# Eight-head retention and a gated MLP on one core: q scaled before its transpose, half-array matmuls, and an order of work computed in the kernel

## The chip, the core and the metric

The kernel runs on one core of a Trainium2 chip. A core has a matrix engine (TensorE, "PE" in the profile; its weight loads are listed as "PEld" and can run beside matmuls), a vector engine (VectorE, "DVE"), a scalar engine (ScalarE, "ACT"), a general engine (GpSimd, "POOL") and SyncE ("SP"), which here only issues transfers. The engines run in parallel, each takes its own instructions in the order of its own list, and they wait for one another on semaphores. The metric is the device time of one execution in microseconds (us): the median of several executions.

## The reference

Batch 8, 8 heads, 576 positions, 64 channels per head. The first half is retention: attention without softmax, in which the score of query position t and key position s is multiplied by gamma^(t-s) for s up to t and by zero above. The second half is a gated MLP that mixes positions with a 576x576 matrix.

```python
scores = scale * np.matmul(q, k.transpose(0, 1, 3, 2))
gamma = 1.0 - 2.0 ** (-5.0 - np.arange(H, dtype=np.float32))
Dmat = np.where(rel >= 0, gamma[:, None, None] ** rel[None, :, :], 0.0)
x = np.matmul(scores * Dmat[None], v)          # then heads side by side: 512 channels
...
h = gelu(x @ w_in)                             # 1024 wide, tanh form
u, v = (h[..., :512], h[..., 512:])
v_n = (v - mean) / np.sqrt(var + 1e-06) * g_ln
v_s = np.einsum('ts,bsd->btd', w_sg, v_n) + b_sg[None, :, None]
return x + (u * v_s) @ w_out
```

## The kernel before

Two batches form a pair of 1152 positions, cut into 9 tiles of 128 positions; there are 4 pairs, so 36 tiles. Tile 4 of a pair (m == MID) holds the last 64 positions of one batch and the first 64 of the next. gamma^(t-s) is split into a factor of t and a factor of s, so that no 576x576 decay matrix is needed: v is multiplied by gamma^(-s) (`gv`, line 220), and the output by gamma^t and the scale (`ttab`, line 275). Earlier tiles enter through a running sum of k^T v per head, kept in a bank of PSUM (`zp`, line 289) and copied out after each tile (`zbd`).

The work of a tile, by line:

- `load` (73 to 75): q, k and v of the tile, 256 KB each in float32, by SP, into a ring of five buffers.
- `prep` (217, 220): POOL casts q and k to bf16 (`qkb`) and multiplies v into `vpad`, where the 64 columns of each head lie in a block of 128 whose other half is zero.
- `attn_T` (234 to 239): PE transposes q and k into one PSUM tile; DVE copies q out (`qT`), and ACT and DVE copy one half each of k into a block-diagonal `kbd`, with zeros in the other half of the rows.
- `attn_S` (251, 253): eight 128x128 matmuls give the scores, each with a contraction of 128 rows of which 64 hold zeros; DVE multiplies by the triangle (`ret`).
- `attn_O` (267, 271, 275): four matmuls from the running sum and eight from `vpad`, all on the whole array; DVE multiplies by `ttab` into `xT`.
- `attn_Z` (289 to 293): the running sum is extended and copied out by DVE and ACT.
- `mlp_V` (307 to 326): four 512-wide matmuls; ACT applies gelu (`vg`), DVE takes mean and variance (`bst`, `mv`), POOL forms the inverse root (`rs`) and the offset (`nm`), ACT normalises into `vn`.
- `mlp_U` (336, 339): sixteen matmuls, gelu on ACT into `uT`.
- `mlp_W` (349, 354): once the five tiles of one batch have their `vn`, the mixing with `w_sg`: per 128 channels, five steps that alternate between two PSUM tiles of 288 positions; DVE multiplies by `uT` into `gT`.
- `mlp_O` (361, 364, 367, 368): eight matmuls per tile, a copy by ACT, and a 256 KB store that ACT's own queue issues.

PSUM has eight banks: one each for `tp`, `ot` and `zp`, two for scores, three (`psD`) shared by `hv`, `hu`, `wp` and `op`. The program issues the functions in a loop over tiles with fixed offsets (prep two tiles ahead, the MLP one behind, two pieces of `mlp_W` or `mlp_O` per turn), and the framework's own scheduler then places the instructions on each engine. `w_sg` is loaded by POOL with a cast (line 190) and transposed by PE in ten groups (`build_wT`, line 205); each of these groups ends with one matmul that uses 64 rows of the array. Rows for g_ln and b_sg are prepared by small DVE operations (lines 97 to 121).

Of the kernel before, what the change touches and what calls it, by code (L numbers as in the profile page):

```python
# [11 lines left out]
F32 = mybir.dt.float32  # L12
# [3 lines left out]
Alu = mybir.AluOpType  # L16


@with_exitstack
def kernel(  # L20
# [18 lines left out]
    NP = B // 2  # L39
    MID = NT // 2  # L40
    HS = S // 2
    SB = (S + 127) // 128
    ORG = S // 2
    lng = [math.log(1.0 - 2.0 ** (-5.0 - i)) for i in range(H)]
# [3 lines left out]
    ld = ctx.enter_context(tc.tile_pool(name="ld", bufs=5))  # L48
    work = ctx.enter_context(tc.tile_pool(name="work", bufs=4))
    pairp = ctx.enter_context(tc.tile_pool(name="pairp", bufs=2))  # L50
    vnp = ctx.enter_context(tc.tile_pool(name="vnp", bufs=10))
    psA = ctx.enter_context(tc.tile_pool(name="psA", bufs=1, space=bass.MemoryType.PSUM))
    psS = ctx.enter_context(tc.tile_pool(name="psS", bufs=2, space=bass.MemoryType.PSUM))
    psD = ctx.enter_context(tc.tile_pool(name="psD", bufs=3, space=bass.MemoryType.PSUM))


    def segs(m):

        if m < MID:
            return [(0, 0, 128 * m, 128)]  # L60
        if m == MID:
            return [(0, 0, 128 * m, S - 128 * m), (S - 128 * m, 1, 0, 128 * (m + 1) - S)]
        return [(0, 1, 128 * m - S, 128)]

    loaded = {}

    def load(i):
        p, m = divmod(i, NT)
        qk = ld.tile([128, 2, H, D], F32, name="qk", tag="qk")
        vf = ld.tile([128, H, D], F32, name="vf")  # L70
        for (p0, b, r0, n) in segs(m):
            bb = 2 * p + b
            nc.sync.dma_start(qk[p0:p0 + n, 0, :, :], q[bb, :, r0:r0 + n, :].transpose([1, 0, 2]))
            nc.sync.dma_start(qk[p0:p0 + n, 1, :, :], k[bb, :, r0:r0 + n, :].transpose([1, 0, 2]))
            nc.sync.dma_start(vf[p0:p0 + n, :, :], v[bb, :, r0:r0 + n, :].transpose([1, 0, 2]))
        loaded[i] = (qk, vf)

    load(0)


    w_in = consts.tile([128, KK, 2 * F2], BF, name="w_in")
    w_out = consts.tile([128, KK, DM], BF, name="w_out")
    wnat = consts.tile([128, SB, S + 128], BF, name="wnat")
    g_col = consts.tile([128, KK], F32, name="g_col")
    w_stage = []
    for half in (1, 0):
        for c in (0, 2):
            wst = ld.tile([128, 2, F2], F32, name="wst", tag="qk")
            nc.sync.dma_start(wst[:], moe_w_in.rearrange("(c p) f -> p c f", p=128)[:, c:c + 2, half * F2:(half + 1) * F2])
            w_stage.append((half, c, wst))  # L90
        load(1 if half else 2)
    nc.sync.dma_start(g_col[:], moe_g_ln.rearrange("(c p) -> p c", p=128))

# [5 lines left out]
    g_tmp = consts.tile([128, KK], F32, name="g_tmp")  # L101
    nonzero(g_col[:], g_tmp[:])
    row4 = consts.tile([4, 2, S], F32, name="row4")
    row4b = consts.tile([4, 2, S], BF, name="row4b")
    row_t = consts.tile([4, S], F32, name="row_t")
    nc.sync.dma_start(row4[:, 0, :F2], moe_g_ln.partition_broadcast(4))
    nc.sync.dma_start(row4[:, 1, :], moe_b_sg.partition_broadcast(4))
    sel_i = consts.tile([4, 1], I32, name="sel_i")
    nc.gpsimd.iota(sel_i[:], pattern=[[0, 1]], base=0, channel_multiplier=1)
    sel = consts.tile([4, 3], F32, name="sel")  # L110

    def build_rows():
        nonzero(row4[:, 0, :F2], row_t[:, :F2])
        nc.vector.reciprocal(row4[:, 0, :F2], row4[:, 0, :F2])
        nc.vector.tensor_copy(sel[:, 0:1], sel_i[:])
        nc.vector.tensor_scalar(sel[:, 1:2], sel[:, 0:1], 2.0, -1.0, op0=Alu.is_ge, op1=Alu.mult)
        nc.vector.scalar_tensor_tensor(sel[:, 2:3], sel[:, 1:2], -2.0, sel[:, 0:1], op0=Alu.mult, op1=Alu.subtract)
        for a, n in ((0, F2), (1, S)):
# [3 lines left out]
        for t in vmid:  # L122
            nc.sync.dma_start(t[0][NB0:NB0 + 4, :], row4b[:, 0, :F2])
            nc.sync.dma_start(t[1][0:4, :], row4b[:, 0, :F2])
        nc.sync.dma_start(wT[0][SB - 1][NB0:NB0 + 4, :], row4b[:, 1, :])
        nc.sync.dma_start(wT[1][0][0:4, :], row4b[:, 1, :])


    ident = consts.tile([128, 128], BF, name="ident")
    make_identity(nc, ident[:])  # L130
    tri = consts.tile([128, 128], BF, name="tri")
    nc.gpsimd.memset(tri[:], 1.0)
    nc.gpsimd.affine_select(tri[:], tri[:], pattern=[[1, 128]],
                            compare_op=Alu.is_ge, fill=0.0, base=0, channel_multiplier=-1)
    tri_mid = consts.tile([128, 128], BF, name="tri_mid")
    NB0 = S - 128 * MID
    nc.vector.tensor_copy(tri_mid[:], tri[:])
    nc.vector.memset(tri_mid[:NB0, NB0:], 0.0)

# [67 lines left out]


    st = {}
    xTs, uTs, gTs = {}, {}, {}  # L210
    zp = {}

    def prep(i):
# [245 lines left out]
```

## Time and profile before

| | us |
|---|---|
| median of 3 runs (273.85 to 275.9) | 273.96 |
| the profiled execution: its span, first to last instruction | 272.1 |
| median less the span: what lies around it | 1.86 |
| PE busy | 227.3 |
| DVE busy | 189.2 |
| ACT busy | 130.1 |
| POOL busy | 128.1 |

The page of the profile gives the busy time of each engine, and the span in 40 slices with the busy share in tenths. Other views group instructions by line (count, busy time, mean duration, and what ended the idle time before them), list the waits, list instructions in order of time, or give the busy time in stretches that the reader chooses. Matmuls are pipelined: the duration of one is longer than the distance from its start to the start of the next, and the latter is what PE can deliver. Of the profiled execution itself no time but the span is given, so the 1.86 us around it are taken from the median.

### The profile page before, as it was taken

To read this page: it belongs to the slowest core of one execution; us is meant where nothing else is said; L and a number is where in the kernel's file an instruction comes from. 1 tells how busy PE (TensorE), PEld (TensorE's weight loads), DVE (VectorE), ACT (ScalarE), POOL (GpSimd) and SP (SyncE) were. 2 spreads that over 40 slices of the span, in tenths; PEclk is the share of its full clock that TensorE was granted. 3 is DMA by queue.
4 is the path that set the end of the run, shared out by engine and by line. 5 is a ranking of instruction groups with operands and counts; after the bars stand their busy time and mean duration, and the time that the engine had idled before them with its cause. 6 is when DMAs were issued, how large, how long until landed. Compare 5 with 4: busy or idle time off the path is not lost.

```text
span 272.1 us, 6371 instructions
## 1 busy us (share of the span) xinstructions
PE 227.3 (84%) x2498; PEld 171.3 (63%) x2498; DVE 189.2 (70%) x405; ACT 130.1 (48%) x230; POOL 128.1 (47%) x244
## 2 busy tenths in 40 slices
PE   0477747869899899987999899879998999889893
PEld 0245534647577687665877677657767877667561
DVE  7766797767786687656865886568777876687140
ACT  1632522344245545554465445565455476644612
POOL 7835316465267456664635575348544551131100
PEclk9999595999999999999999999999999999999998
DMA  7999999099403799398949789596966022100314
GB/s 167 273 290 232 221 198 229 4 209 193 83 4 104 200 219 213 111 279 214 193 119 211 166 168 263 167 225 126 221 173 149 2 77 80 40 4 0 116 62 173
DMA packets 120606, 42.02 MB, mean 154 GB/s; under 512 B 113824, under 2 KB 114424, under 8 KB 120576
## 3 DMA queue, kind: packets, MB, share of 16 engines
q1 hardware_dynamic: 114736, 31.51, 57.6%
q10 hardware_dynamic: 5184, 9.44, 9.5%
q0 software_dynamic: 656, 0.66, 1.4%
q8 instruction: 19, 0.31, 0.6%
q14 instruction: 11, 0.09, 0.1%
HBM read 32.80 MB, written 9.44 MB: 155 GB/s over the span
## 4 chain that ended last, share of the span: by engine, by line
PE 39%; DVE 22%; ACT 11%; DMA 8%; POOL 7%; issue 6%; SPq 3%; ACTq 2%; POOLq 0%; DVEq 0%
PE hv L307 7%; PE wp L349 6%; PE op L361 6%; PE hu L336 5%; DVE bst L312 5%; DMA vf<-in_v_dram 4%; ACT ob L367 4%; DVE xT L275 4%; ACT vg L310 4%; PE tp L234 3%; PE sc L251 3%; PE ot L271 3%; POOL rs L317 2%; ACTq L368 2%; DVE kbd_169 L239 2%
## 5 line engine op out<-in xcount | busy, mean ns | idle before, releaser
L316 POOL TENSOR_SCALAR rs<-mv 128x1 f32<-128x1 f32 x36 | 8.0, 223 | 110.0 <-DVE mv L314 105.1
L326 ACT ACTIVATE vn<-vg,nm,rs 128x512 bf16<-128x512 f32 x32 | 26.0, 814 | 50.7 <-POOL nm L319 50.7
L253 DVE TENSOR_TENSOR ret<-sc,tri 128x512 bf16<-128x512 f32 x64 | 41.0, 682 | 10.9 <-PE sc L251 10.9
L307 PE MATMUL hv<-w_in,xT 128*128 128x512 bf16 x144 | 40.3, 398 | 3.8 <-DVE xT L275 3.7
L217 POOL CAST qkb<-qk 128x1024 bf16<-128x1024 f32 x36 | 37.2, 1032 | 10.8 <-DMA qk<-in_k_dram 7.1
L312 DVE BATCH_NORM_STATS2 bst<-vg 128x6 f32<-128x512 f32 x36 | 25.0, 694 | 24.7 <-ACT vg L310 24.0
L336 PE MATMUL hu<-xT,w_in 128*128 128x128 bf16 x576 | 38.8, 221 | 1.3 <-ACT ob L367 1.3
L310 ACT ACTIVATE vg<-hv 128x512 f32<-128x512 f32 x36 | 21.5, 597 | 36.6 <-PE hv L307 30.5
L336 PEld LDWEIGHTS <-w_in 128*128 128x128 bf16 x576 | 35.1, 99 | 4.0 <-issue 2.5
L361 PE MATMUL op<-w_out,gT 128*128 128x512 bf16 x144 | 36.9, 379 | 0.0
L349 PEld LDWEIGHTS <-vn 128*128 128x128 bf16 x256 | 24.4, 97 | 18.9 <-issue 11.8
L354 DVE TENSOR_TENSOR gT<-wp,uT 128x288 bf16<-128x288 f32 x64 | 26.1, 448 | 11.3 <-PE wp L349 11.3
L234 PEld LDWEIGHTS <-qkb 128*128 128x128 bf16 x288 | 20.2, 103 | 15.5 <-POOL qkb L217 7.5
L234 PE MATMUL tp<-ident,qkb 128*128 128x128 bf16 x288 | 23.7, 229 | 6.7 <-POOL qkb L217 6.5
L275 DVE TENSOR_TENSOR xT<-ot,ttab 128x512 bf16<-128x512 f32 x36 | 24.9, 691 | 6.1 <-PE ot L271 5.4
L367 ACT ACTIVATE ob<-op 128x512 f32<-128x512 f32 x36 | 21.1, 592 | 11.2 <-PE op L364 7.2
L339 ACT ACTIVATE uT<-hu 128x512 bf16<-128x512 f32 x36 | 21.2, 590 | 10.3 <-PE hu L336 10.2
L317 POOL TENSOR_TENSOR rs<-rs,mhalf 128x1 f32<-128x1 f32 x36 | 20.6, 571 | 2.7
L307 PEld LDWEIGHTS <-xT 128*128 128x128 bf16 x144 | 12.5, 101 | 12.9 <-DVE xT L275 5.2
L236 DVE COPY qT<-tp 128x512 bf16<-128x512 bf16 x36 | 15.0, 417 | 7.2 <-PE tp L234 6.9
L361 PEld LDWEIGHTS <-gT 128*128 128x128 bf16 x144 | 12.7, 98 | 8.8 <-DVE gT L354 0.3
L364 PEld LDWEIGHTS <-xT 128*128 128x128 bf16 x144 | 11.1, 98 | 8.4
(135 smaller groups left out, 440.9 us busy)
## 6 DMA issues: line engine op xcount, KB each, us to landing
out_dram<-ob ACTq DMA_DIRECT2D x36, 256.0 KB, 2.2
qk<-in_q_dram SPq DMA_DIRECT2D x32, 256.0 KB, 4.8
qk<-in_k_dram SPq DMA_DIRECT2D x32, 256.0 KB, 4.6
vf<-in_v_dram SPq DMA_DIRECT2D x32, 256.0 KB, 4.9
wst<-in_moe_w_in_dram SPq DMA_DIRECT2D x4, 512.0 KB
wst<-in_moe_w_out_dram SPq DMA_DIRECT2D x2, 512.0 KB
qk<-in_q_dram SPq DMA_DIRECT2D x8, 128.0 KB, 5.8
qk<-in_k_dram SPq DMA_DIRECT2D x8, 128.0 KB
```

What stands on the lines that cost most here:

```text
L217: nc.gpsimd.tensor_copy(qkb[:], qk[:].rearrange("p a h d -> p a (h d)"))
L234: nc.tensor.transpose(tp[:, a, kk, :], s["qkb"][:, a, kk * 128:(kk + 1) * 128], ident[:])
L253: nc.vector.tensor_tensor(ret[:, 4 * j:4 * j + 4, :], sc[:], msk[:].unsqueeze(1).to_broadcast([128, 4, 128]), op=Alu.mult)
L275: nc.vector.tensor_tensor(xTs[p][:, :, 128 * m:128 * m + 128], ot[:], ttab[:, :, t0:t0 + 128], op=Alu.mult)
L307: nc.tensor.matmul(hv[:], xTs[p][:, kk, 128 * m:128 * m + 128], w_in[:, kk, F2:], start=(kk == 0), stop=(kk == KK - 1))
L310: nc.scalar.activation(vg[:], hv[:], Act.Gelu_apprx_tanh)
L312: nc.vector.bn_stats(bst[:], vg[:])
L336: nc.tensor.matmul(hu[:, c, :], w_in[:, kk, 128 * c:128 * c + 128], xTs[p][:, kk, 128 * m:128 * m + 128], start=(kk == 0), stop=(kk == KK ...
L349: nc.tensor.matmul(ps[half][:], vns[t0 + j][e][:, 128 * c:128 * c + 128], wT[e][j][:, half * HS:(half + 1) * HS], start=(j == 0), stop=(j ...
L354: nc.vector.tensor_tensor(gTs[p][:, c, col:col + HS], ps[half][:], uTs[p][:, c, col:col + HS], op=Alu.mult)
L361: nc.tensor.matmul(op[:], gTs[p][:, c, r], w_out[:, c, :], start=(c == 0), stop=False, skip_group_check=True)
L367: nc.scalar.activation(ob[:], op[:], Act.Copy)
```

## The change

The attention half is rewritten, several operations move to other engines, and the order of all instructions is computed in the kernel.

- q is multiplied by gamma^t and the scale before it is transposed (`qs`, on POOL), so the output needs no `ttab`; ACT copies it to `xT`. k is cast by ACT (`kb`) rather than by POOL.
- The transposed q and k are copied out of PSUM by one DVE operation of 1024 columns (`qkT`). There is no block-diagonal k: the scores of even heads use rows 0 to 63 of the array, those of odd heads rows 64 to 127, and the two write different PSUM banks.
- v is not padded: an even head's output uses columns 0 to 63 of the array, an odd head's columns 64 to 127, so they write the two halves of one PSUM tile.
- The running sum is copied out by ACT alone. The normalisation `vn` moves from ACT to POOL, as (vg - mean) * rs, and the addition of 1e-6 from POOL to DVE.
- The mixing forms one half of 288 positions after the other, each in a bank of its own; the product overwrites `uT`.
- Stores are issued by SP, in one list with the loads; `w_sg` is loaded by SP as float32 and cast by ACT.
- The framework's scheduler is switched off (`tc.manual_schedule()`). The kernel describes each piece of work as a unit with an engine, a cost, a key (a due time, in steps of 5300 ns per tile), what it reads and writes, and the PSUM banks it takes. The class `Plan` then plays the units through: at each step it takes the engine that can start first and, among that engine's units that can start by then, the one with the lowest key. Instructions are emitted in that order.

```diff
+    def emit(self):
...
+        for _ in units:
+            t, e = min((max(free[e], min(start(n) for n in r)), e) for e, r in ready.items() if r)
+            n = min((m for m in ready[e] if start(m) <= t), key=lambda m: (units[m][2], m))
...
+            free[e] = t + cost
+            done = t + cost + self.HOP[e]
...
+            emit(*([[s[1] for s in held[n]]] if take is not None else
+                   [[held[m][w][1] for m, which in give for w in which]] if give is not None else []))
...
+        plan.add("ACT", 600, key + 1, lambda: nc.scalar.activation(
+            kb[a][:], qkf[l][:, 1, :, :].rearrange("p h d -> p (h d)"), Act.Copy),
+                 reads=rd(i, 1), writes=[("kb", a)])
+        plan.add("POOL", 1220, key, lambda: nc.gpsimd.tensor_tensor(
+            qs[a][:].rearrange("p (h d) -> p h d", h=H), qkf[l][:, 0, :, :], gq[:, m, :].unsqueeze(2).to_broadcast(bc), op=Alu.mult),
+            reads=rd(i, 0) + ["gq"], writes=[("qs", a)])
+        plan.add("POOL", 1220, key + 2, lambda: nc.gpsimd.tensor_tensor(
+            vb[a][:], vf[l][:], gv[:, m, :].unsqueeze(2).to_broadcast(bc), op=Alu.mult),
+            reads=rd(i, 2) + ["gv"], writes=[("vb", a)])
...
+        plan.add("DVE", 650, key, lambda banks: nc.vector.tensor_copy(
+            qkT[r][:].rearrange("p a k c -> p (a k c)"), banks[0][:]),
+            reads=[("tpu", i)], writes=[("qkT", r)], give=[(u, [0])])
...
-            for r in range(4):
-                kk, hh = 2 * j + r // 2, r % 2
-                nc.tensor.matmul(sc[:, r, :], s["kbd"][:, kk, hh, :], s["qT"][:, kk, :],
-                                 start=True, stop=True, skip_group_check=True)
+            for kk in range(KK):
+                for hh in range(2):
+                    sl = slice(hh * 64, hh * 64 + 64)
+                    nc.tensor.matmul(banks[hh][:, kk, :], qkT[r][sl, 1, kk, :], qkT[r][sl, 0, kk, :],
+                                     start=True, stop=True, skip_group_check=True)
...
-            for hh in range(2):
-                nc.tensor.matmul(ot[:, kk, :], s["vp"][:, 2 * kk + hh, :], s["ret"][:, 2 * kk + hh, :],
-                                 start=first, stop=(hh == 1), skip_group_check=True)
+            for kk in range(KK):
+                for hh in range(2):
+                    nc.tensor.matmul(ot[hh * 64:hh * 64 + 64, kk, :], vb[a][:, 2 * kk + hh, :], ret[r][hh][:, kk, :],
+                                     start=(m == 0 and kk == 0), stop=True, skip_group_check=True)
...
-        nc.vector.tensor_tensor(xTs[p][:, :, 128 * m:128 * m + 128], ot[:],
-                                ttab[:, :, t0:t0 + 128], op=Alu.mult)
+        plan.add("ACT", 600, key + 8, lambda banks: nc.scalar.activation(
+            xT[p % NX][:, :, 128 * m:128 * m + 128], banks[0][:], Act.Copy),
+            reads=[("otu", i)], writes=[("xT", p % NX, m)], give=[(u, [0])])
...
-            nc.scalar.activation(vn[:], vg[:], Act.Identity, scale=rs[:], bias=nm[:])
+            nc.gpsimd.tensor_tensor(st[:, 8:9], st[:, 8:9], mhalf[:], op=Alu.pow)
...
+                nc.gpsimd.tensor_scalar(dst[sl, :], vg[g][sl, :], st[sl, 6:7], st[sl, 8:9],
+                                        op0=Alu.subtract, op1=Alu.mult)
...
-                nc.tensor.matmul(ps[half][:], vns[t0 + j][e][:, 128 * c:128 * c + 128],
-                                 wT[e][j][:, half * HS:(half + 1) * HS],
...
+                        nc.tensor.matmul(banks[0][:, :HS], src[:, 128 * c:128 * c + 128],
+                                         wT[e][j][:, half * HS:(half + 1) * HS],
...
-        nc.scalar.dma_start(outf[128 * i:128 * i + 128, :], ob[:])
+            plan.add("SP", 400, key, lambda i=i: nc.sync.dma_start(outf[128 * i:128 * i + 128, :], ob[i % NO][:]),
+                     reads=[("ob", i % NO)], writes=[("out", i)], dma=720)
...
+    with tc.manual_schedule():
+        plan.emit()
```

More of the change, by code (lines that the diff above doesn't have):

```diff
@@ L54, with sb @@
[L54 removed]
+    psum = ctx.enter_context(tc.tile_pool(name="psum", bufs=1, space=bass.MemoryType.PSUM))
+    def sb(name, shape, dt=BF):
+        return consts.tile(shape, dt, name=name)
+    NL, NQ, NR, NX, NO, NG = 5, 3, 3, 2, 4, 4
+    qkf = [sb(f"qkf{i}", [128, 2, H, D], F32) for i in range(NL)]
+    vf = [sb(f"vf{i}", [128, H, D], F32) for i in range(NL)]
+    qs = [sb(f"qs{i}", [128, H * D]) for i in range(NQ)]
@@ L78 @@
[L78 to L91, printed above, removed]
@@ new lines @@
+    tables()
+    g_and_b()
+    for n, (half, c) in enumerate(((1, 0), (1, 2), (0, 0), (0, 2))):
+        w_load(half, c, n)
+    load(0)
+    for i in range(N):
+        if i:
+            load(i)
+        if i == 2:
+            weights()
+        attention(i)
+        if i:
+            mlp_V(i - 1)
+            mlp_U(i - 1)
+        if i and (i - 1) % NT == MID:
+            batch(2 * ((i - 1) // NT))
+        if i and (i - 1) % NT == NT - 1:
+            batch(2 * ((i - 1) // NT) + 1)
+    mlp_V(N - 1)
```

595 lines of the change are left out of this document (318 added, 277 removed).

## The prediction

> **What bounds the kernel now.** The page comes first, then the stretches of the span, then PE's instructions in order of time.
>
> ```profile
> span 272.1 us, 6371 instructions
> PE 227.3 (84%) x2498; PEld 171.3 (63%) x2498; DVE 189.2 (70%) x405; ACT 130.1 (48%) x230; POOL 128.1 (47%) x244
> ```
>
> ```profile
> 0.00:20.00 20.00, 7.50 (x52) 5.25 (x53) 14.32 (x41) 8.13 (x17) 13.09 (x30) 1.00 1.03 244
> 20.00:45.00 25.00, 15.91 (x154) 11.83 (x152) 21.17 (x40) 7.66 (x14) 9.67 (x16) 0.80 1.07 221
> 45.00:75.00 30.00, 24.59 (x271) 18.27 (x272) 21.26 (x45) 12.01 (x22) 15.16 (x26) 0.94 0.71 130
> 75.00:250.00 175.00, 162.65 (x1896) 125.63 (x1895) 127.96 (x272) 94.51 (x166) 88.24 (x168) 1.00 0.65 145
> 250.00:272.10 22.10, 16.69 (x130) 10.32 (x128) 4.46 (x11) 7.75 (x13) 1.90 (x6) 0.96 0.29 108
> ```
>
> The columns are the stretch, its length, busy time (and count) of PE, PEld, DVE, ACT and POOL, granted clock, DMA share, GB/s. There are two kernels in one span. From 75 us to 250 us PE is busy 162.65 of 175. Before 75 us it is busy 48.0 of 75, while the DMA engines are full (1.03, 1.07) until 45 us: there it waits for data and for chains. So the questions are how much PE work there is, how early PE fills, and how much it loses once full. The work is read from starts that follow without a gap:
>
> ```profile
> 130.85 0.39 PE L289 MATMUL zp<-vpad_164,qkb 128*128 128x128 bf16 x4
> 131.08 0.41 PE L349 MATMUL wp<-wT_0_191,vn 128*128 128x288 bf16 x2
> ...
> 132.30 0.29 PE L349 MATMUL wp<-wT_0_191,vn 128*128 128x288 bf16 x1
> ...
> 133.81 0.61 PE L251 MATMUL sc<-qT,kbd_169 128*128 128x128 bf16 x8
> 134.25 1.03 PE L307 MATMUL hv<-w_in,xT 128*128 128x512 bf16 x4
> 135.12 0.61 PE L234 MATMUL tp<-ident,qkb 128*128 128x128 bf16 x8
> 135.56 1.06 PE L336 MATMUL hu<-xT,w_in 128*128 128x128 bf16 x16
> 136.46 0.22 PE L267 MATMUL ot<-qT,zbd_170 128*128 128x128 bf16 x1
> ...
> 137.12 1.03 PE L361 MATMUL op<-w_out,gT 128*128 128x512 bf16 x4
> ...
> 138.21 0.38 PE L361 MATMUL op<-w_out,gT 128*128 128x512 bf16 x1
> ```
>
> Start to start: running sum 0.23 us, scores 0.44, hv 0.87, transposes 0.44, hu 0.90, output 0.66 (12 matmuls at 0.055), op 1.09, and ten wp in 1.22 (131.08 to 132.30). The 36 tiles of scores, hv, transposes, hu and op make 36 x 3.74 = 134.6; outputs 32 x 0.66 + 4 x 0.44 (a pair's first tile has no running sum) = 22.9; sums 32 x 0.23 = 7.4; 320 wp 39.0. The ten groups that transpose w_sg take 0.46 each:
>
> ```profile
> 64.19 0.52 PE L205 MATMUL wtp<-ident,wnat 128*128 128x128 bf16 x5
> 64.65 0.30 PE L349 MATMUL wp<-wT_2_193,vn 128*128 128x288 bf16 x1
> ```
>
> That is 4.6. **PE's work is 208.5 us** at the full clock; the other 63.6 of the span are waiting, clock and edges.
>
> **The change, part by part.** *Half-array matmuls.* Scores and the v part of the output are eight 0.055 us matmuls each. If the two halves of each pair run at once, a tile saves 0.22 on either: 36 x 0.44 = 15.8. If they run one after the other they save nothing. No row of this trace shows two halves at work; I take the full saving, since nothing but their place differs from matmuls that follow one another, and keep the other end for the range. Their cost stands in the 0.46 above. Its fifth matmul is the one that uses 64 rows:
>
> ```profile
> L205 PE MATMUL wtp<-ident,wnat 64*128 64x64 bf16 x10 | 2.1, 209 | 0.0
> ```
>
> Four at 0.055 and one of half the columns would be 0.25, so going to half the rows and back costs 0.21, 0.105 per switch. In the compiled order of the changed kernel the array's shape changes 156 times: 20 in the w_sg groups, which exist before too, and 136 new ones (some outputs stand next to scores and share one). 136 x 0.105 = 14.3; the low end is 0, if eight matmuls hide what one could not. I take the row. PE's work is then 208.5 - 15.8 + 14.3 = **207.0**: the halves pay for their own switches and no more. The Trainium skill, "TensorEngine Tiling (Array Packing)", Key Properties, says that different tiles of the array can load weights and multiply in parallel; no run here shows that yet, and by it the full saving holds.
>
> *What moves between engines*, from rows grouped by line:
>
> ```profile
> L253 DVE TENSOR_TENSOR ret<-sc,tri 128x512 bf16<-128x512 f32 x64 | 41.0, 682 | 10.9 <-PE sc L251 10.9
> L354 DVE TENSOR_TENSOR gT<-wp,uT 128x288 bf16<-128x288 f32 x64 | 26.1, 448 | 11.3 <-PE wp L349 11.3
> L326 ACT ACTIVATE vn<-vg,nm,rs 128x512 bf16<-128x512 f32 x32 | 26.0, 814 | 50.7 <-POOL nm L319 50.7
> L312 DVE BATCH_NORM_STATS2 bst<-vg 128x6 f32<-128x512 f32 x36 | 25.0, 694 | 24.7 <-ACT vg L310 24.0
> L310 ACT ACTIVATE vg<-hv 128x512 f32<-128x512 f32 x36 | 21.5, 597 | 36.6 <-PE hv L307 30.5 <-PE hu L336 2.3 <-PE ot L271 1.3
> L317 POOL TENSOR_TENSOR rs<-rs,mhalf 128x1 f32<-128x1 f32 x36 | 20.6, 571 | 2.7
> L236 DVE COPY qT<-tp 128x512 bf16<-128x512 bf16 x36 | 15.0, 417 | 7.2 <-PE tp L234 6.9
> L293 ACT ACTIVATE zbd_171<-zp 64x256 bf16<-64x256 f32 x16 | 6.1, 379 | 7.7 <-DVE zbd_171 L292 7.4
> L217 POOL CAST qkb<-qk 128x1024 bf16<-128x1024 f32 x36 | 37.2, 1032 | 10.8 <-DMA qk<-in_k_dram 7.1 <-PE tp L234 3.6
> L220 POOL TENSOR_TENSOR vpad_163<-vf,gv 128x256 bf16<-128x256 f32 x16 | 9.5, 612 | 0.0
> L114 DVE RECIPROCAL row_111<-row_111 4x512 f32<-4x512 f32 x1 | 3.3, 3330 | 0.0
> ```
>
> Per tile afterwards. DVE: the copy of 1024 lies between 0.42 and 0.83 (one and two of L236), say 0.67; two masks 1.36; statistics 0.69 and about 0.3 for two tiny operations; gT 64/36 x 0.448 = 0.80: 3.8 us. POOL: q and v scaled, twice two of L220, 2.45; the power 0.57; vn between 0.52 (half a cast) and 1.22 (two of L220), say 0.9: 3.9. ACT: cast of k between 0.60 and 0.81, xT, vg, uT and ob about 0.6 each, two half copies of the sum 0.76: 3.8 to 4.0. PE needs 207.0/36 = 5.75, so all this stands beside PE and I cost it at nothing once PE is full; POOL would bind only if vn took 2.7 us. What goes is a queue: ACT no longer stands 50.7 us behind POOL's nm with evacuations of PSUM queued behind it.
>
> *Start.* In the compiled order PE's first wp stands behind the transposes of the ninth tile, so PE cannot be full before q and k of that tile are there. The bytes ahead of them in SP's list: eight tiles at 0.786 MB, 0.52 of the ninth, w_in 2.10, w_out 1.05, w_sg 1.33: 11.3 MB. The stretches above moved 244 x 20 + 221 x 25 = 10.4 MB by 45 us; 0.9 more at 221 GB/s gives 49 us, and one POOL multiply 50. DVE, with 3.33 for the reciprocal and its neighbours now ahead of the first copy, has about 46 us of work until then: it ends near the same point, so this cover is thin, and each us that DVE comes later adds one. PE work before that wp: 9 transposes 4.0, 8 sums 1.8, 8 scores 1.8, 7 outputs 2.9, 7 hv and hu 12.4, the w_sg groups 4.6, 30 switches 3.1: 30.6. Left: 176.4.
>
> *Full stretch.* Before, PE loses 175 - 162.65 = 12.35 us here (7.1%), and what it waits for is:
>
> ```profile
> PE wp L349 <- DVE gT L354: 5.9, 6, 1.1
> PE wp L349 <- ACT vg L310: 1.7, 4, 0.5
> PE ot L267 <- ACT zbd_170 L293: 1.3, 2, 0.9
> PE hu L336 <- ACT ob L367: 1.3, 3, 0.5
> ```
>
> The first is a wp pair that needs two of three banks at once, the second and fourth are ACT's late evacuations: 8.9 us whose cause is edited away (one bank per group, no vn on ACT). Left are 3.5, plus the gaps that pipelined ends conceal: the work in those 175 us, by its counts at the rates above, is about 158, so up to 9.6% is lost. I take 4%, with 2% and 9.6% as ends: 176.4/0.96 = 183.8.
>
> *Stores in SP's list.* A store waits for its ob, and the loads behind it wait too. They run four tiles ahead (five buffers), some 23 us; I cost it at nothing while that lasts; after that every us that SP stands is one that PE waits.
>
> *End.* After the last hv the mixing needs gelu, statistics and vn, 0.6 + 1.0 + 1.5, of which hu covers 0.9: 2.5 us with hops. After PE's end, as before:
>
> ```profile
> 267.32 0.39 PE L364 MATMUL op<-ident,xT 128*128 128x128 bf16 x4
> ```
>
> which leaves 272.1 - 267.7 = 4.4. **Sum: 50 + 183.8 + 2.5 + 4.4 = 240.7**, against the profiled 272.1; with the 1.86 us by which the median 273.96 exceeds that span, 242.6.
>
> **The rivals.** *Cheap switches.* At half the price the switches cost 7.2 less, the start ends at 47, 2% are lost: 47 + (176.4 - 5.6)/0.98 + 6.9 + 1.9 = 230. For it: eight matmuls per visit. Against: the row. *Order out of step.* The planned order is fixed; where a real duration differs, engines wait in an order that was right for another time. If the loss stays 9.6%: 195.1 instead of 183.8, so 254. For it: before, SP already stood behind stores,
>
> ```profile
> SPq L74 <- DMA out_dram<-ob: 37.0, 6, 16.8
> ```
>
> up to 16.8 us at once. *Halves in turn*: the change then does not do what it says, PE keeps its 15.8, 16.5 at 96%: 259. *Column loads.* Each of the 288 column-half matmuls loads its own weights, 103 ns by
>
> ```profile
> L234 PEld LDWEIGHTS <-qkb 128*128 128x128 bf16 x288 | 20.2, 103 | 15.5 <-POOL qkb L217 7.5 <-issue 0.6 <-POOL kmid L226 0.3
> ```
>
> Before, loads hide behind matmuls. If they stand open, a matmul costs 0.103 instead of 0.0275: 288 x 0.0755 = 21.7, 22.6 at 96%: 265. The Trainium skill, same page, Restrictions, says that column tiling disables the fast weight load, which speaks for this; no run here shows it. *Every alternation drains*, the one that ends slower: heads alternate between halves, 7 times in each group of eight, 36 x 14 = 504 times in all. If each alternation costs a switch, 504 x 0.105 = 52.9 and the 15.8 of overlap is lost: 68.7/0.96 = 71.6 on top, 314. With the overlap lost it turns slower than before above 0.03 us per alternation. For it: a change of rows did cost 0.105. Against: the shape stays, only the place moves.
>
> **How the numbers follow.** Forecast 242.6 (its own range 233 to 250): 0.50. Cheap switches 230: 0.16. Out of step 254: 0.10. In turn 259: 0.08. Column loads 265, with its upper part within 1% of before: 0.06. Alternation 314: 0.10. The range 225 to 264 leaves out the last, most of the column loads and the fast edge of the cheap switches, about 0.18. Within 1%, 271.2 to 276.7, is about what a measurement of this kernel can tell from no change. Faster: 0.50 + 0.16 + 0.10 + 0.08 + 0.03 = 0.87; same 0.03; slower 0.10.
>
> **What the profile of the changed kernel would show.** Scores: eight starts span 0.22 us plus about 0.1 at either side if the sum is right, 0.44 and more if the halves take turns, above 1 us if each alternation drains. Output: the same behind the running sum. PE full from about 50 us; if it fills later, the first wp's releaser says whether data, DVE or POOL was late. After that, idle of PE near 4%, with POOL at about 3.9 us per tile and ACT without waits for POOL. The forecast is wrong if PE's list is blocked by POOL (a vn far above 0.9 us), if SP's stores starve the loads, or if switches cost other than 0.105.

## The result and the profile after

The changed kernel takes **252.09 us** (median of 4 runs, 248.24 to 252.97) against 273.9 us for the kernel before (median of 4, 273.51 to 275.9): a ratio of 0.910, with a 95% interval of 0.900 to 0.920. Some executions fall into a slower state, and the ratios leave them out (two of the four after, 252.81 and 252.97), which is why this one is not the 0.920 of the two medians. The forecast was 242.6 us, with a range of 225 to 264. The profiled execution took 251.38 us, its span is 249.7, so 1.7 us lie around it, as before (1.86).

The head of the page, and the span in the stretches that the prediction used (stretch, length, busy time and count of PE, PEld, DVE, ACT, POOL, granted clock, DMA share, GB/s), of the changed kernel:

```profile
span 249.7 us, 6386 instructions
PE 217.8 (87%) x2498; PEld 153.0 (61%) x2498; DVE 155.7 (62%) x328; ACT 135.0 (54%) x267; POOL 178.5 (71%) x158
```

```profile
0.00:20.00 20.00, 6.09 (x46) 3.56 (x48) 17.62 (x35) 7.75 (x24) 7.65 (x15) 1.00 0.92 229
20.00:45.00 25.00, 19.40 (x262) 13.98 (x259) 17.50 (x39) 14.75 (x29) 17.21 (x15) 0.99 1.07 239
45.00:75.00 30.00, 25.62 (x285) 17.82 (x285) 18.39 (x36) 15.89 (x31) 26.31 (x23) 0.95 1.05 193
75.00:225.00 150.00, 148.97 (x1790) 106.72 (x1788) 97.46 (x209) 90.35 (x174) 122.60 (x103) 1.00 0.68 161
225.00:249.70 24.70, 17.71 (x127) 10.95 (x125) 4.70 (x11) 6.25 (x11) 4.74 (x4) 0.86 0.23 86
```

Three things differ from before. In the full stretch PE stands 1.03 us of 150 (0.7%), where it stood 12.35 of 175 (7.1%). From 20 to 45 us it does more (262 matmuls, 154 before). And the last 25 us run at a granted clock of 0.86. What PE waits for over the whole span (us in all, times, longest):

```profile
PE p_tp L345 <- POOL qs L335: 9.1, 3, 6.0
PE p_s L356 <- DVE qkT L348: 5.6, 5, 4.4
PE p_d L455 <- POOL vn L422: 4.4, 4, 3.4
PE p_z L370 <- POOL vb L338: 4.4, 5, 1.6
```

6.0 us of the first row are the wait for the first data. From 75 to 225 us, the full stretch, a single row is left, and none of those that the prediction showed for before (gT, vg, zbd, ob):

```profile
PE p_d L455 <- POOL vn L422: 1.0, 3, 0.4
```

The groups whose durations the prediction had to bound (busy, mean ns of one):

```profile
L422 POOL TENSOR_SCALAR vn<-vg,stat 128x512 bf16<-128x512 f32 x32 | 66.5, 2078 | 3.3
L335 POOL TENSOR_TENSOR qs<-qkf,gq 128x512 bf16<-128x512 f32 x36 | 38.4, 1067 | 12.4 <-DMA qkf<-in_q_dram 9.8 <-PE p_tp L345 2.4
L348 DVE COPY qkT<-p_tp 128x1024 bf16<-128x1024 bf16 x36 | 24.7, 686 | 11.1 <-PE p_tp L345 10.9
L422 POOL TENSOR_SCALAR vmid<-vg,stat 64x512 bf16<-64x512 f32 x8 | 16.6, 2074 | 0.8
```

vn takes 2.08 us on POOL, not the 0.9 that I took and outside the bounds of 0.52 and 1.22. The middle tile's two halves of 64 partitions cost as much each, 4.2 together. The copy of 1024 (0.69) lies where its bounds put it.

The half-array matmuls, in PE's order of time (start, length, then the group):

```profile
126.44 1.06 PE L435 MATMUL p_d<-xT,w_in 128*128 128x128 bf16 x16
127.43 0.41 PE L390 MATMUL p_ot<-ret,vb 128*64 128x128 bf16 x8
127.78 0.40 PE L356 MATMUL p_s<-qkT 64*128 64x128 bf16 x8
128.11 0.82 PE L475 MATMUL p_d<-w_out,uT 128*128 128x512 bf16 x3
...
132.72 0.39 PE L386 MATMUL p_ot<-qkT,zbd 128*128 128x128 bf16 x4
133.04 0.41 PE L390 MATMUL p_ot<-ret,vb 128*64 128x128 bf16 x8
133.39 0.30 PE L455 MATMUL p_d<-wT,vmid 128*128 128x288 bf16 x1
```

Eight outputs take 0.35 us start to start and eight scores 0.33, each with one switch, against 0.44 on the whole array. The hu before them (126.44) takes 0.99 instead of 0.90, with the first switch: the three switches together cost 0.33 us, 0.11 each. The output with its four running products takes 0.67 (132.72 to 133.39), against 0.66 before: the halves save 0.22 and pay it back in switches, as forecast.

The start. PE, POOL and SP's queue around the first wp, each in order of time:

```profile
60.42 0.40 PE L345 MATMUL p_tp<-ident,qs 128*128 128x128 bf16 x4 [1.13 <-POOL qs L335]
...
60.88 0.65 PE L455 MATMUL p_d<-wT,vn 128*128 128x288 bf16 x4
```

```profile
50.31 4.23 POOL L422 TENSOR_SCALAR vmid<-vg,stat 64x512 bf16<-64x512 f32 x2
...
57.28 2.08 POOL L422 TENSOR_SCALAR vn<-vg,stat 128x512 bf16<-128x512 f32 x1
59.33 1.04 POOL L335 TENSOR_TENSOR qs<-qkf,gq 128x512 bf16<-128x512 f32 x1
```

```profile
44.97 1.09 SPq L201 DMA_DIRECT2D qkf<-in_q_dram  x1
...
49.65 1.05 SPq L321 DMA_DIRECT2D vmid<-row4b  x1
...
53.41 0.58 SPq L324 DMA_DIRECT2D wT<-row4b  x1
54.08 0.39 SPq L201 DMA_DIRECT2D vf<-in_v_dram  x1
```

The first wp comes at 60.9 us, not at 50. The ninth tile's q was issued at 44.97 and lands some 4.6 us later (the median of the loads issued from 45 to 62 us), so the data was there at 50, as forecast. But POOL scales it only at 59.33, behind 9.7 us of its own work without a gap, and the wp stand behind its transposes in PE's list. SP issues no load from 49.65 to 54.08: it issues the six small transfers that put the rows of g_ln and b_sg into vmid and wT. DVE had finished these rows before 19 us (L280).

Some of the start is the clock. The granted clock is 0.50 from about 44.7 to 48.0 us, and hv, from 45.77 to 47.48, takes 1.71 us instead of 0.87:

```profile
45.40 0.59 PE L370 MATMUL p_z<-vb,kb 128*128 128x128 bf16 x4 [1.63 <-POOL vb L338]
45.77 1.91 PE L405 MATMUL p_d<-w_in,xT 128*128 128x512 bf16 x4
47.48 1.32 PE L435 MATMUL p_d<-xT,w_in 128*128 128x128 bf16 x16
```

The end, on PE:

```profile
229.23 0.53 PE L455 MATMUL p_d<-wT,vn 128*128 128x288 bf16 x3
233.15 0.42 PE L455 MATMUL p_d<-wT,vn 128*128 128x288 bf16 x1 [3.39 <-POOL vn L422]
...
233.61 1.17 PE L455 MATMUL p_d<-wT,vn 128*128 128x288 bf16 x4
...
240.50 1.03 PE L475 MATMUL p_d<-w_out,uT 128*128 128x512 bf16 x4
...
245.71 0.39 PE L478 MATMUL p_d<-ident,xT 128*128 128x128 bf16 x4
```

PE stands 3.39 us for the last vn. Then four wp take 1.17 us instead of 0.65, for some 6 us, at a granted clock of 0.50: 36 wp last 7.35 us (233.15 to 240.50) where 36 x 0.1225 = 4.41 would do.

Against the forecast's sum of 240.7, then: first wp 60.9 - 50 = +10.9; from there to PE's end 246.1 - 60.9 = 185.2, of which 3.39 + 2.94 belong to the end, so 178.9 for the 176.4 of work, against 183.8: -4.9; the end 6.3 against 2.5: +3.8; behind PE's end 3.6 against 4.4: -0.8. Together +9.0, which is 249.7 - 240.7.

### The profile page after: what moved, and what is told of

Its sections match the earlier page's. It is cut to its first block, busy times and chain, and to the rows that moved or that the text cites. A ratio compares the mean times of both kernels' runs of the same rounds, so it can differ in the third digit from the quotient of the medians.

```text
span 249.7 us, 6386 instructions
## 1 busy us (share of the span) xinstructions
PE 217.8 (87%) x2498; PEld 153.0 (61%) x2498; DVE 155.7 (62%) x328; ACT 135.0 (54%) x267; POOL 178.5 (71%) x158
## 4 chain that ended last, share of the span: by engine, by line
PE 55%; POOL 19%; issue 9%; SPq 6%; DMA 5%; ACT 3%; POOLq 1%; ACTq 0%
PE p_d L455 15%; PE p_d L475 9%; PE p_d L435 8%; PE p_d L405 7%; POOL vn L422 7%; POOL vb L338 4%; PE p_tp L345 4%; SPq L201 4%; DMA vf<-in_v_dram 3%; PE p_ot L390 3%; POOL vmid L422 3%; POOL stat L419 3%; POOL qs L335 3%; PE p_s L356 3%; PE p_d L478 2%
## 5 line engine op out<-in xcount | busy, mean ns | idle before, releaser
L422 POOL TENSOR_SCALAR vn<-vg,stat 128x512 bf16<-128x512 f32 x32 | 66.5, 2078 | 3.3
L361 DVE TENSOR_TENSOR ret<-p_s,tri 128x512 bf16<-128x512 f32 x64 | 42.6, 685 | 33.6 <-PE p_s L356 33.5
L455 PE MATMUL p_d<-wT,vn 128*128 128x288 bf16 x256 | 43.6, 299 | 4.4 <-POOL vn L422 4.4
L335 POOL TENSOR_TENSOR qs<-qkf,gq 128x512 bf16<-128x512 f32 x36 | 38.4, 1067 | 12.4 <-DMA qkf<-in_q_dram 9.8
L338 POOL TENSOR_TENSOR vb<-vf,gv 128x512 bf16<-128x512 f32 x36 | 38.1, 1059 | 6.3 <-PE p_ot L390 5.1
L405 PE MATMUL p_d<-w_in,xT 128*128 128x512 bf16 x144 | 38.8, 394 | 0.2
L463 DVE TENSOR_TENSOR uT<-p_d,uT 128x288 bf16<-128x288 f32 x64 | 28.3, 454 | 16.7 <-PE p_d L455 16.5
L435 PE MATMUL p_d<-xT,w_in 128*128 128x128 bf16 x576 | 38.5, 220 | 0.0
L475 PE MATMUL p_d<-w_out,uT 128*128 128x512 bf16 x144 | 37.1, 380 | 0.0
L413 DVE BATCH_NORM_STATS2 stat<-vg 128x6 f32<-128x512 f32 x36 | 24.8, 689 | 12.8 <-ACT vg L408 12.8
L348 DVE COPY qkT<-p_tp 128x1024 bf16<-128x1024 bf16 x36 | 24.7, 686 | 11.1 <-PE p_tp L345 10.9
```

What stands on the lines that cost most here:

```text
L335: plan.add("POOL", 1220, key, lambda: nc.gpsimd.tensor_tensor(qs[a][:].rearrange("p (h d) -> p h d", h=H), qkf[l][:, 0, :, :], gq[:, m, :] ...
L338: plan.add("POOL", 1220, key + 2, lambda: nc.gpsimd.tensor_tensor(vb[a][:], vf[l][:], gv[:, m, :].unsqueeze(2).to_broadcast(bc), op=Alu.mult),
L348: plan.add("DVE", 650, key, lambda banks: nc.vector.tensor_copy(qkT[r][:].rearrange("p a k c -> p (a k c)"), banks[0][:]), reads=[("tpu", ...
L361: plan.add("DVE", 650, key + 4, lambda banks, hh=hh: nc.vector.tensor_tensor(ret[r][hh][:], banks[0][:], msk[:].unsqueeze(1).to_broadcast( ...
L405: nc.tensor.matmul(banks[0][:], xT[p % NX][:, kk, 128 * m:128 * m + 128], w_in[:, kk, F2:], start=(kk == 0), stop=(kk == KK - 1))
L413: nc.vector.bn_stats(st[:, 0:6], vg[g][:])
```

## The experiments

Theories for the 9 us. **A**: POOL's vn at 2.08 us holds both start and end. **B**: the start is held by the loads and by DVE, and POOL only looks late there. **C**: the planner's wrong price for vn put the order out of step. After the first four runs B was narrowed to a cause that the first expectations had not named: the six small transfers of the rows, which stand in SP's list behind the loads of nine tiles. Beside these stands the question what made the kernel faster at all. Ratios are to the kernel before in the same session; the changed kernel itself has 0.910 (0.900 to 0.920). Times differ by about 1% from run to run, so the traces decide where the medians are close.

**vn on DVE.**

```diff
-                nc.gpsimd.tensor_scalar(dst[sl, :], vg[g][sl, :], st[sl, 6:7], st[sl, 8:9],
+                nc.vector.tensor_scalar(dst[sl, :], vg[g][sl, :], st[sl, 6:7], st[sl, 8:9],
...
-        plan.add("POOL", 1870 if m == MID else 1220, key + 2, norm, reads=[("vg", g), ("st", g), "vmid0", "srow"],
+        plan.add("DVE", 900 if m == MID else 450, key + 3, norm, reads=[("vg", g), ("st", g), "vmid0"],
```

> Edit: the two-scalar normalisation vn moves from POOL to DVE (planned at 450 ns), the power stays on POOL; the planner orders the new units. Theory A (the missing 9 us are POOL's vn, 2.08 us where the prediction had 0.9): POOL busy falls by about 83 us to 95, DVE rises by about 18 to 174; the first wp starts at 50 to 54 us instead of 61; the idle of PE behind vn after 205 us goes; the span falls from 249.7 to 235 to 240. Rival B (the start is held by the loads and by DVE, POOL only looks late): first wp stays at 58 us or later, the span gains under 4 us. Rival C (the planner's wrong costs put the order out of step): a gain no larger than that of the run which only corrects the cost.

Measured: 246.05 us (244.51 to 248.81), ratio 0.892 (0.884 to 0.901), some 5 us less by the ratios: more than B expected, and much less than A. The profiled execution took 2.8 us more than the median, so only places and single durations are read from it. The wait at the end falls to 1.65 us and its wp run at full speed. But the start does not move forward:

```profile
63.37 0.67 PE L457 MATMUL p_d<-wT,vn 128*128 128x288 bf16 x4
```

This first wp is even later than 60.88, with one tile more of other work ahead of it in the list, and its row shows no wait for POOL or any other engine: PE only comes to it then. A holds for the end and falls for the start.

**The same kernel, with the planner told what vn costs on POOL.**

```diff
-        plan.add("POOL", 1870 if m == MID else 1220, key + 2, norm, reads=[("vg", g), ("st", g), "vmid0", "srow"],
+        plan.add("POOL", 4780 if m == MID else 2640, key + 2, norm, reads=[("vg", g), ("st", g), "vmid0", "srow"],
```

> Edit: vn stays on POOL, but the planner is told what it takes (2640 ns for power and vn, 4780 for the tile with two parts) instead of 1220 and 1870. Theory A (the work itself holds the start and the end): within 4 us of 249.7 either way, first wp at 58 us or later. Rival C (order out of step with real durations): the span falls by 6 us or more, with POOL's busy time unchanged at about 178.

Measured: 249.7 us (246.68 to 251.98), ratio 0.904 (0.894 to 0.914): 1 to 2 us at best, inside the scatter. The clock of the stretch from 225 to 240 us is 0.77, as without the edit. That the order was planned with a wrong price for vn (C) is not the main cause.

**Stores on ACT's queue.**

```diff
-            plan.add("SP", 400, key, lambda i=i: nc.sync.dma_start(outf[128 * i:128 * i + 128, :], ob[i % NO][:]),
+            plan.add("ACT", 60, key, lambda i=i: nc.scalar.dma_start(outf[128 * i:128 * i + 128, :], ob[i % NO][:]),
```

> Edit: the stores are issued by ACT's queue again, all else as in the changed kernel. If stores in SP's list hold the loads behind them (the chain of the changed kernel passes a store and then a v load at 120 to 125 us), the span falls by 2 to 5 us. As predicted (loads run four tiles ahead): within 2 us of 249.7.

Measured: 250.54 us (248.08 to 251.24), ratio 0.908 (0.898 to 0.917), no difference. In the planned order the stores in SP's list cost nothing, as forecast.

**Scores and outputs on the whole array.**

```diff
-                    nc.tensor.matmul(banks[hh][:, kk, :], qkT[r][sl, 1, kk, :], qkT[r][sl, 0, kk, :],
+                    nc.tensor.matmul(banks[hh][:, kk, :], qkT[r][:, 1, kk, :], qkT[r][:, 0, kk, :],
...
-                    nc.tensor.matmul(ot[hh * 64:hh * 64 + 64, kk, :], vb[a][:, 2 * kk + hh, :], ret[r][hh][:, kk, :],
+                    nc.tensor.matmul(ot[:, kk, :], vb[a][:, 2 * kk:2 * kk + 2, :].rearrange("p g c -> p (g c)"), ret[r][hh][:, kk, :],
...
```

> Edit: scores and the v part of the output use the whole array again, as many matmuls as before, the layout of the data kept (each product then mixes the two heads of a pair, so the values are others; count and size of all operations stay). Theory (the halves just pay for their switches): a group of eight takes 0.44 us start to start and no switch, so PE's work changes by -14.3 + 15.8 = +1.5 us and the span by 0 to 3 us. Rival (the halves are worth more than their switches): 6 us or more slower. Rival (the switches cost more): 5 us or more faster.

Measured: 251.36 us (251.15 to 251.84), ratio 0.914 (0.907 to 0.921). On PE:

```profile
128.43 0.61 PE L390 MATMUL p_ot<-ret,vb 128*128 128x128 bf16 x8
128.88 0.61 PE L356 MATMUL p_s<-qkT 128*128 128x128 bf16 x8
```

0.45 us for eight outputs, without a switch, against 0.35 with its switch. The times do not differ beyond their intervals: most of what the half arrays save goes into the switches. That it is all of it is not shown, because the profiled executions lost unlike amounts to the clock. Here the clock did not fall at 45 us, and the last 36 wp took 6.1 us (234.88 to 240.97) instead of 7.35. Without these some 2.4 us the halves would be ahead by about 2 to 3 us, an estimate from the two spans (250.1 and 249.7).

**Four forms of vn on POOL**, one for each pair of batches.

```diff
+                if p == 0:
+                    nc.gpsimd.tensor_scalar(dst[sl, :], vg[g][sl, :], st[sl, 6:7], st[sl, 8:9],
+                                            op0=Alu.subtract, op1=Alu.mult)
+                elif p == 1:
+                    nc.gpsimd.tensor_scalar(dst[sl, :], vg[g][sl, :], st[sl, 8:9], None, op0=Alu.mult)
+                elif p == 2:
+                    nc.gpsimd.tensor_scalar(dst[sl, :], vg[g][sl, :], 0.1, 3.0, op0=Alu.subtract, op1=Alu.mult)
+                else:
+                    n = sl.stop - sl.start
+                    nc.gpsimd.tensor_tensor(dst[sl, :], vg[g][sl, :], st[sl, 8:9].to_broadcast([n, F2]), op=Alu.mult)
```

> What makes vn cost 2.08 us on POOL? The four pairs of batches take four forms of the same 128x512 instruction: pair 0 as in the changed kernel (subtract a per-partition scalar, multiply by a per-partition scalar), pair 1 one multiply by one per-partition scalar, pair 2 subtract and multiply with two constants, pair 3 a two-tensor multiply by a broadcast column, the form of qs and vb. Pairs 1 to 3 compute something else than the normalisation. If each arithmetic step costs 2 ns per element: 2.08, 1.04, 2.08, 1.06 us. If each per-partition scalar costs it and constants are cheap: 2.08, 1.0 to 1.3, below 1.0, 1.06. If the cost hangs on the instruction and not on its operands: 2.08, 2.08, 2.08, 1.06. The time is expected at 244 to 252 us, between the kernel with vn on DVE and the changed one.

Measured, as groups by line:

```profile
L423 POOL TENSOR_SCALAR vn<-vg,stat 128x512 bf16<-128x512 f32 x8 | 16.6, 2077 | 0.9
L428 POOL TENSOR_SCALAR vn<-vg 128x512 bf16<-128x512 f32 x8 | 15.4, 1929 | 0.7
L426 POOL TENSOR_SCALAR vn<-vg,stat 128x512 bf16<-128x512 f32 x8 | 12.6, 1571 | 0.8
L431 POOL TENSOR_TENSOR vn<-vg,stat 128x512 bf16<-128x512 f32 x8 | 8.3, 1040 | 0.6
```

None of the three expectations fits alone. Two constants in place of two columns save 0.15 us, one step in place of two saves 0.51, and the two-tensor form with a broadcast column does one step in 1.04. So it is mainly the instruction: it is slow on POOL with either kind of operand. The time of the one execution, 429.76 us where 244 to 252 was expected, says nothing of the forms: PE ran at about half speed throughout (four hv in 1.78 us, 205.69 to 207.47, instead of 0.87), though the granted clock is recorded as 1.00. POOL's qs and vb took 1.04 and 1.05 us there, as in the changed kernel, so its durations can be read.

**The order left to the framework.** The same units in the same order of the program, but each compute engine's list ordered anew, as in the kernel before.

```diff
-    with tc.manual_schedule():
-        plan.emit()
+    plan.emit()
```

> The same units handed over in the planner's order, but each engine's list is then ordered anew by the framework's own scheduler, as in the kernel before. If the planner's order on each engine is what brought the loss in the full stretch from 7.1% to 0.7%, the loss comes back: 6% of 178 us, 11 us, so 258 to 266. If the loss went because vn is off ACT and one bank serves each group (my two causes), the order matters little: 249 to 256.

Measured: 301.9 us (300.73 to 303.06), ratio **1.093** (1.086 to 1.101): slower than before, by far more than either theory gave. What SP waits for most:

```profile
SPq L484 <- ACT ob L482: 88.3, 27, 11.6
```

SP's list is still almost the planned one, with stores between loads, but the other engines now come to the stores at other times; SP stands 88.3 us behind them in all, where it stands 63.7 in the changed kernel. I had taken the two edits of my own list (vn off ACT, one bank per group) as the cause of the smaller loss. By themselves they are not enough. Part of the loss is the clock, which is 0.94 from 75 to 250 us and 0.65 from 45 to 75.

**And with the stores on ACT's queue**, as in the earlier run.

> As the kernel without the fixed order (301.9 us), with the stores issued by ACT's queue, so that SP's list holds loads alone. There SP stood 88.3 us in all behind stores whose ob was late. If the planner's order is worth so much because it keeps SP's loads ahead of the work, most of the loss goes: 255 to 275. If the order on PE, DVE and POOL itself is what counts, it stays above 285.

Measured: 281.34 us (280.71 to 282.89), ratio 1.016 (1.013 to 1.020). The stretches of both kernels, first without and then with this edit:

```profile
75.00:250.00 175.00, 156.23 (x1687) 106.10 (x1688) 89.31 (x195) 85.13 (x168) 118.59 (x103) 0.94 0.63 142
```

```profile
45.00:75.00 30.00, 18.51 (x151) 12.72 (x152) 13.10 (x27) 8.60 (x17) 14.42 (x12) 0.65 0.55 117
75.00:225.00 150.00, 137.67 (x1550) 97.75 (x1574) 83.08 (x181) 80.76 (x156) 114.06 (x98) 0.94 0.75 166
```

Neither bound was met. 20.6 of the 49.8 us between 301.9 and 252.1 go with the stores; 29.2 stay with the order on the other engines, the lower clock (0.94 from 75 to 225 us) included: PE does 151 matmuls from 45 to 75 us where the changed kernel does 285, and stands idle for 8% of the time from 75 to 225 us. So the new division of the work, without the planned order, is no faster than the kernel before. Whether a planned order alone would have made the old division faster wasn't tried.

**The rows' transfers on ACT's queue**, with vn on DVE.

```diff
-                nc.sync.dma_start(t[0][NB0:NB0 + 4, :], row4b[:, 0, :F2])
-                nc.sync.dma_start(t[1][0:4, :], row4b[:, 0, :F2])
...
+                nc.scalar.dma_start(t[0][NB0:NB0 + 4, :], row4b[:, 0, :F2])
+                nc.scalar.dma_start(t[1][0:4, :], row4b[:, 0, :F2])
...
-        plan.add("SP", 2600, 4.5 * T0, put, reads=["rows2", "rows3", "vmid0"],
+        plan.add("ACT", 3600, 4.0 * T0, put, reads=["rows2", "rows3", "vmid0"],
-                 writes=[("wT", 0, SB - 1), ("wT", 1, 0), "vmid_g"], dma=200)
+                 writes=[("wT", 0, SB - 1), ("wT", 1, 0), "vmid_g"])
```

> vn on DVE, and the six small transfers of the rows of g_ln and b_sg, which the mixing needs, issued by ACT's queue instead of SP's. If the mixing starts late because these transfers stand in SP's list behind the loads of nine tiles (which puts the first wp behind the ninth tile's transposes in PE's list), the first wp comes at 54 to 58 instead of 63.4 us and the time falls to 241 to 244. If the start is bound by data and by DVE's weight work, the first wp moves in the list, PE idles elsewhere instead, and the time stays within 1.5 us of 246.

Measured: **243.44 us** (243.25 to 244.64), ratio 0.882 (0.877 to 0.888), the fastest of all. The first wp starts at 52.65 us instead of 63.37, and from 50 to 100 us PE is busy without a gap:

```profile
50.00:75.00 25.00, 25.00 (x284) 17.33 (x281) 18.62 (x38) 14.93 (x29) 14.81 (x16) 0.95 1.11 212
```

The planner counts a transfer in SP's list as landed only after all loads ahead of it. The rows, issued behind the loads of nine tiles, therefore made the wp late in the plan, and the plan put them behind the ninth tile's transposes. Played through with its own costs, the changed kernel's plan has the fifth tile's vn done at 45.4 us, the rows landed at 52.5, and the first wp at 52.5. They were late on the chip too: SP issued the last of them at 53.41. Off SP's list, and without the `dma=200` that put them into the planner's queue, they come before: ACT issues them from 36.1 to 40.3 us.

**The same, with DVE relieved at the start**: w_in cast by POOL, g_col and w_out scaled later, some of the last ops kept for the end.

```diff
-        plan.add("DVE", 700, early, lambda: nc.vector.tensor_copy(
+        plan.add("POOL", 1032, early, lambda: nc.gpsimd.tensor_copy(
...
-                plan.add("DVE", 450, kw + 1 * T0, lambda c=c, s=s, r=r: nc.vector.tensor_scalar(
+                plan.add("DVE", 450, 8 * T0, lambda c=c, s=s, r=r: nc.vector.tensor_scalar(
```

> As the one before, and in addition w_in is cast by POOL instead of DVE, g_ln's column work and the scaling of w_out move behind the eighth tile in DVE's list, and the first-half ops of the last pair are kept for the end. If DVE's list of weight work is what holds the attention of tiles 4 to 6 at 40 to 50 us, the time falls to 236 to 241. If the loads hold the start (11.3 MB at some 230 GB/s end at 49 us), it gains at most 1 us over the one before.

Measured: 244.98 us (244.36 to 246.06), ratio 0.887 (0.880 to 0.894): no gain over the one before. The first wp stays at 52.4 us, so DVE's list of weight work is not what is left of the start.

**The two losses apart**, in the changed kernel with vn on POOL: the rows alone on ACT's queue (the edit of **The rows' transfers on ACT's queue**); the very last vn alone on DVE; both.

```diff
+        last = i == N - 1
...
-                nc.gpsimd.tensor_scalar(dst[sl, :], vg[g][sl, :], st[sl, 6:7], st[sl, 8:9],
+                (nc.vector if last else nc.gpsimd).tensor_scalar(dst[sl, :], vg[g][sl, :], st[sl, 6:7], st[sl, 8:9],
...
```

> The changed kernel with vn left on POOL, and only the six small transfers of the g_ln and b_sg rows issued by ACT's queue. In the changed kernel POOL's vn of the fifth tile was done at 54.5 us and the first wp came at 60.9. If the place of the rows in SP's list set the order that kept the first wp behind the ninth tile, it now comes at 54.5 to 56 us and the time falls by 3 to 5 us against 252.1: 247 to 249. If POOL's 2.08 us per vn alone holds the start, PE stands for POOL at another place and the time stays at 250 to 252.

> The changed kernel with the vn of the very last tile alone moved to DVE. In the changed kernel PE stands 3.39 us for that vn and then runs 36 wp in 7.51 us instead of 4.4. If the end costs that much, PE's wait falls to 1.7 us, the wp take 4.4 to 4.6, and the time falls by 4 to 5 us: 247 to 248. If the slow wp have another cause than the wait before them, it falls by 1.7 us only: 250.4.

> Both edits at once, with the other 35 vn left on POOL. If start and end are separate losses, their gains add up: 242 to 245, as fast as all vn on DVE with the rows on ACT's queue (243.4), and POOL's 2.08 us per vn costs nothing between the two. If POOL also holds the full stretch, it stays 2 us or more behind 243.4.

Measured: the rows alone 247.24 us (246.96 to 248.18), ratio 0.897 (0.891 to 0.904); the last vn alone 247.73 (246.62 to 249.2), 0.899 (0.892 to 0.905); both 243.93 (243.03 to 246.66), 0.886 (0.879 to 0.893). The profiled spans are 245.7, 245.1 and 242.2, against 249.7: -4.0, -4.6 and -7.5. By the ratios the gains are 1.3, 1.1 and 2.4% of before's time. Taken alone, the first two lie inside the scatter of the changed kernel; together they are clear of it, and they add up nearly. With the rows alone, PE and POOL:

```profile
50.33 0.67 PE L455 MATMUL p_d<-wT,vn 128*128 128x288 bf16 x4
51.28 0.30 PE L455 MATMUL p_d<-wT,vmid 128*128 128x288 bf16 x1 [0.28 <-POOL vmid L422]
```

The first wp starts at 50.33 us, though vn still takes 2.08 on POOL; its fifth matmul waits 0.28 us for POOL and no more. So the start was the rows' place, not POOL's speed. The edit brings the rows earlier, frees SP for loads and changes the order, all at once; what each is worth was not tried apart. With the last vn alone:

```profile
231.52 0.30 PE L461 MATMUL p_d<-wT,vn 128*128 128x288 bf16 x1 [1.79 <-DVE vn L428]
231.78 0.65 PE L461 MATMUL p_d<-wT,vn 128*128 128x288 bf16 x4
```

The wait is 1.79 us and the wp behind it run at 0.65 for four at once: the slow wp went with the long wait. And both edits, with 35 vn left on POOL, are as fast as all vn on DVE (243.9 and 243.4): between start and end POOL's vn costs next to nothing.

## Why the prediction was right, and where it was off

The direction, the range and most of the size came out; 9.5 us separate forecast and median. One of the prediction's own signs of being wrong came true, a vn far above 0.9 us: it cost at the end, and 1.0 us of waits in the full stretch.

- **PE's work, 207.0 us**: right. The halves overlap, and the switches (0.105 each by before's w_sg row) take back what they save. The rows show it (0.11 measured per switch), and the whole-array kernel agrees within its interval, which leaves room for 2 to 3 us either way. The rule of the Trainium skill that I used for the overlap ("TensorEngine Tiling (Array Packing)", Key Properties) agrees with the 0.33 us for eight scores with a switch, against 0.44.
- **What moves between engines, costed at nothing**: right for the full stretch, though one term was far off. vn measured 2.08 us, not 0.9, and my two bounds (half a cast, two of L220) were both multiplies and casts, none of them this form. POOL needs 1.07 + 1.06 + 0.56 + 2.08 = 4.8 us per tile (two more on the middle tile), under PE's 5.75, so it doesn't bind, as the 2.7 us limit said.
- **Start, 50 us**: the step that failed. The data term was right: the ninth tile's q was there at 50. Wrong was to take the place of the first wp, behind the ninth tile's transposes, as a fact to be priced by bytes alone. Between the data and those transposes stood POOL's vmid and vn, and the reason for the place, six small transfers in SP's list, I did not count at all: neither the 4.4 us in which SP issues no load, nor that they decide the order. It cost 10.9 us at the first wp, of which the runs give back some 4 in time. The 50 us also took the full clock for granted; half of it from 44.7 to 48.0 us is a term that the sum does not have.
- **Full stretch, 4% lost**: too much; 1.4% by the same sum, which gave back 4.9 us. The low end of 2% was still too high. And the reason I gave was not sufficient: with the same division and banks, but without the planned order, PE stands idle there for 8% of the time (75 to 225 us, stores on ACT's queue) and 11% (75 to 250 us, stores in SP's list). The planned order is what keeps the loss small. I had argued only from before's waits and took the order as a risk.
- **Stores in SP's list at nothing**: right in the planned order. The condition I set (loads far enough ahead) is what failed in the kernel without it, at 20.6 us.
- **End, 2.5 us**: mis-sized. The wait is 3.39 instead of some 2.5 because vn is 1.2 us longer than taken, and the clock then costs 2.94 more, a term that I had not written.
- **The rivals.** Switches are not cheap: 0.11 each. Alternating halves do not drain, and the halves do not take turns: eight scores in 0.33, with a switch. Column loads do not stand open: eight column-half matmuls take 0.35 with their switch, where open loads of 103 ns would need 0.82. The rule in the Trainium skill, same page, Restrictions, that column tiling disables the fast weight load, brings no cost that these rows show. An order out of step with real durations cost little: told the right price for vn, the planner gained 1 to 2 us at most.

## What to carry to other kernels

When a program orders all lists, read its order as a result of its prices: ask of each instruction with a late place which modelled wait put it there, and count the small transfers in a queue as well as the large ones. A chain at the very end of a kernel costs its length and can cost the clock behind it too: here 3.39 us of waiting and 2.94 of slow matmuls. And before an operation moves to another engine, look for a row of that engine with the same instruction and operands; a row of a like operation bounds nothing.

## What the runs showed of the hardware

- A tensor_scalar of 128x512 on POOL takes 1.57 us with one step and 1.93 (constants) to 2.08 (columns) with two, and as long with 64 partitions as with 128 (2074 and 2078 ns); a tensor_tensor takes 1.04.
- The granted clock fell to 0.50 around long waits of PE, but not by their length alone. In the changed kernel it fell during the wait of 3.39 us at the end, and PE then ran at half speed for some 6 us (four wp in 1.17). It also fell at about 44.7 us, in a wait of 1.63, with waits of 0.55, 0.23 and 0.22 just before. After 1.65 and 1.79 us at the end of the two kernels with the last vn on DVE it did not fall. In the whole-array kernel, behind the same 3.39 us, it fell only about 1 us after PE had begun again, and was back some 3.4 us later:

```profile
235.13 0.65 PE L455 MATMUL p_d<-wT,vn 128*128 128x288 bf16 x4
...
236.84 1.17 PE L455 MATMUL p_d<-wT,vn 128*128 128x288 bf16 x4
```

The Trainium skill, "TensorE: Matmul & The Clock Gate", Part 1, says that the clock is halved after an idle window of about 3.4 us and comes back after as long a busy one. The two waits of 3.39 us are about that long; the fall in a wait of 1.63 us does not fit, and the 6 us at half speed are longer. What sets the fall stays open here.

- The same DVE instruction was slower beside POOL. With vn on DVE:

```profile
23.02 1.26 DVE L424 TENSOR_SCALAR vn<-vg,stat 128x512 bf16<-128x512 f32 x1
...
29.18 0.54 DVE L424 TENSOR_SCALAR vn<-vg,stat 128x512 bf16<-128x512 f32 x1
```

At 23.02 POOL works on vb and qs, at 29.18 it is idle (from 28.7 to 31.9). The scaling of w_out takes 1054 ns on average in the changed kernel and 474 with vn on DVE. That the shared access of the two engines is the reason wasn't tried apart.
